# Attention with top-32 masking and two expert stages on one core: the first routed expert's slots in two passes, the first pass from the tokens of the first eight blocks

## The chip, the cores and the metric

The kernel runs on one core of a Trainium2 chip. The metric is the device time of one execution in microseconds (us). The engines are TensorE (PE in the rows, its weight loads PEld), VectorE (DVE), ScalarE (ACT), GpSimd (POOL) and SyncE (SP), which here only issues transfers.

## The reference, cut to what matters

Three stages follow one another on 2304 tokens of width 512. The change touches the third, and the end of the second.

```python
def _moe_ref(x, w_in, w_out):            # second stage, 2048 wide
    h = x @ w_in
    return (h * np.clip(h + 3, 0, 6) / 6) @ w_out

def _moe2_ref(x, w_gate, w1, w2):        # third stage: E = 8 experts, F = 1024
    logits = x @ w_gate
    expert_idx = np.argmax(logits, axis=1)
    gate_w = softmax(logits)[np.arange(N), expert_idx]
    for e in range(E):
        mask = expert_idx == e
        h = np.maximum(x[mask] @ w1[e], 0.0)
        out[mask] = gate_w[mask, None] * (h @ w2[e])
```

Each token goes to one expert alone. Which one is known only when the token's row of the second stage is complete.

## The kernel before, in words

**Tiling.** Tokens are worked in nine blocks of 256 (TB); each block has two tiles of 128. The main loop (lines 1075 to 1131) runs over attention tiles, and takes one step of the second stage in each turn. The second loop (lines 1143 to 1156) takes the steps that are left, without attention. A step (`moe_step`, line 1017) works on one of 16 slices of the hidden width of a block: `l1` (line 842) is 12 matmuls of 256 columns, `l2` (line 874), three steps behind, is 6 matmuls of 512 columns into the two banks `yps`. Every product is made of three matmuls, high by high, high by low, low by high. Between the two, ScalarE, VectorE and GpSimd make the activation and split it in two parts (`epi_a`, `epi_b`, `epi_c`); the parts gh and gl have two buffers each.

**Gates.** When a block's 16 steps are done, `yevac` (line 884) copies `yps` to two tiles `ysb` (three buffers), and a generator `gate` (line 893) per tile follows: four transposes and their copies, four small matmuls for the logits, the largest, its index, the one-hot row, a prefix count in its expert (lines 934 and 935), the token's row to DRAM (`yd`), and its number to a place in a table in DRAM (`td`, an indirect write of GpSimd, line 960). `gate_step` moves each generator one yield on; the loops call it once a turn. For the last block the table's entries are also made on chip (`place`, `in128`), and its indirect writes wait in a list, `tables`.

**Table and gather.** `load_table` reads the DRAM table back (`trow`) when the gates of the first 16 tiles are done. Behind the second loop, the counts give the experts' ranks (lines 1169 to 1175), and matmuls with `trow` and the last block's entries give `tab` and `tabg`: for each expert three slots of 128 token numbers (lines 1176 to 1185). Expert 0 always has the first rank; the others follow by count, and SP reads their numbers into registers (line 1189) for the addresses of their weights. `xgather` (line 1193) fetches the token rows of an expert by indirect reads of GpSimd, `xprep` (line 1204) transposes a slot's rows and splits them.

**Experts.** ROOM (line 98) says how many slots a rank has: 384, 384, 352, 320 three times, 256 twice. A step of an expert takes one of 8 slices (F = 1024): `m2l1` (line 1218) is 12 matmuls with as many columns as the rank has slots, `m2l2` (line 1239), two steps behind, 3 matmuls of 512 columns for each slot group. `m2out` scales, and writes the rows out by indirect writes. An expert's weights come as 8 pieces of 512 KB: `wload_` (line 985) loads one into one of three `raw` buffers, `wpiece` (line 998) splits it into a high part (ScalarE) and a low part (VectorE). Expert 0's first six pieces are loaded and split during the last 13 steps of the second stage; expert e + 1's piece f is asked for at step f of expert e.

**What sets the order.** The code doesn't write the order of each engine's queue out. Each instruction gets a priority number (`pr`, line 146: the turn's base and an offset by kind, gates 525, `l1` 310, `l2` 260, a turn is 400), and a planner builds every queue ahead of time: of the instructions whose inputs and buffers are there by the planner's own estimates, the one with the lowest number is next. On the chip a queue is worked in that order, and an instruction whose input is late holds up those behind it.

Of the kernel before, what the change touches and what calls it, by code (L numbers as in the profile page):

```python
# [57 lines left out]
def attention_two_moe_kernel(  # L58
# [38 lines left out]
    NSL = NE * SLOTS  # L97
    ROOM = [CAP, CAP, CAP - 32] + [CAP - 64] * 3 + [CAP - P] * 2

    def slots(r):  # L100
        return -(-ROOM[r] // P)

    def slot(r, j):
        return min(P, ROOM[r] - j * P)
    NCK = 8
# [114 lines left out]
    def body(cs, exact):  # L220
# [9 lines left out]
        m1p = m1.enter_context(tc.tile_pool(name="m1p" + X, bufs=1))  # L230
        ps1 = m1.enter_context(tc.tile_pool(name="ps1" + X, bufs=1, space=PSUM))
        at = ExitStack()
# [28 lines left out]

        wih = m1p.tile([P, NCC, F1], F32R, name="wih")
        wil = m1p.tile([P, NCC, F1], F32R, name="wil")

# [628 lines left out]
        def gate(bk, tt, y):  # L893
# [52 lines left out]
            if last:  # L946

                ad2 = m1p.tile([P, 1], I32, tag="ad2", bufs=2, name=f"ad2{i}")
                place, in128 = [wp[0].tile([P, n], F32, tag=f"oh{n}", bufs=2, name=f"oh{n}_{i}") for n in (P, NSL)]
# [26 lines left out]


        NPC = 4
        FW = F2 // NPC
# [18 lines left out]
        def wpiece(e, i):  # L998
            kind, pc = i % 2, i // 2
            if (e, i) not in wraw:  # L1000
                wload_(e, i)
            raw = wraw.pop((e, i))
            late = kind and pc >= NPC // 2
            nb = 3 if kind else 5
            pool = tabp[0] if late else wp[0]
            h = pool.tile([P, 4 * FW], F32R, tag=f"wh{kind}", bufs=nb, name=f"wh{e}_{i}")
            l = pool.tile([P, 4 * FW], F32R, tag=f"wl{kind}", bufs=nb, name=f"wl{e}_{i}")
# [135 lines left out]
        while gpos[0] < NG + 3 or pend:  # L1143
            pr0[0] += STEP
            run(moe_step())
            gate_step()
            tc.cur_priority = pr0[0] + STEP
            if gdone[0] == NTT - TB // P and not trows:
                load_table()
            if gpos[0] > NG - 13 and len(pre) < NPC + NPC // 2:  # L1150

                if len(wraw) == 3 or len(pre) + len(wraw) == NPC + NPC // 2:
                    pre.append(order[len(pre)])
                    wpiece(0, pre[-1])
                if len(pre) + len(wraw) < NPC + NPC // 2:
                    wload_(0, order[len(pre) + len(wraw)])
        m1.close()
# [4 lines left out]
        ps2 = m2.enter_context(tc.tile_pool(name="ps2" + X, bufs=1, space=PSUM))  # L1162
# [4 lines left out]
        rk = ps2.tile([P, 256], F32, name="rk")  # L1167
        cnt = rk[0:NSL, 0:NE]
        PE.matmul(cnt, ones[:, 0:NSL], ohsum, start=True, stop=True)
# [5 lines left out]
        V.tensor_scalar(place_, cs["row"][0:NSL, 0:NSL], rank[:, 2:3], None, op0=ALU.is_equal)  # L1175
        tq = ps2.tile([NSL, P], F32, tag="tp", bufs=2, name="tq")
        for i, a_ in enumerate(trows):
# [3 lines left out]
        V.scalar_tensor_tensor(trows[0], tq, part[:, 3:4], cs["row"][0:NSL, :], op0=ALU.subtract, op1=ALU.subtract)  # L1181
        tps = ps2.tile([P, NSL], F32, tag="tp", bufs=2, name="tps")
# [3 lines left out]
        PE.matmul(rk[0:1, 16:16 + NE], part[:, 1:2], place_.rearrange("p (e s) -> p e s", s=SLOTS)[:, :, 0], start=True, stop=True)  # L1186
        V.tensor_copy(cs["list"], rk[0:1, 16:16 + NE])
        for r in range(1, NE):
# [4 lines left out]
        def xgather(e):  # L1193
# [4 lines left out]
            for j in range(slots(e)):  # L1198
                x = tabp[0].tile([P, YW], F32, tag="xg", bufs=4, name=f"xg{e}_{j}")[0:slot(e, j)]
                G.indirect_dma_start(x, None, yd, bass.IndirectOffsetOnAxis(tabg[0:slot(e, j), e * SLOTS + j:e * SLOTS + j + 1], 0))  # L1200
                xg.append(x)
            xst[e] = (xh, xl, gw, xg)

        def xprep(e, j):
            xh, xl, gw, xg = xst[e]
            x = xg[j]
            m = slot(e, j)
            tp = ps2.tile([P, NCC, P], F32, tag="tp", bufs=2, name=f"tp{e}_{j}")[:, :, 0:m]
            for c in range(NCC):
# [8 lines left out]
        def m2l1(e, f):  # L1218
# [4 lines left out]
            fs = slice((f % FPP) * P, (f % FPP + 1) * P)  # L1223
            w = ROOM[e]
            lp = ps2.tile([P, CAP], F32, tag="lp", bufs=2, name=f"lp{e}_{f}")[:, 0:w]
# [10 lines left out]

        ops_ = [ps2.tile([P, DM], F32, name=f"ops{j}") for j in range(SLOTS)]

# [9 lines left out]
        def m2out(e):  # L1248
            gw = xst[e][2]
            for j in range(slots(e)):  # L1250
                m = slot(e, j)
                o = tabp[0].tile([P, DM], F32, tag="osb", bufs=3, name=f"osb{e}_{j}")[0:m]
                A.activation(o, ops_[j][0:m], AF.Copy, scale=gw[0:m, j:j + 1])
                si = G.indirect_dma_start(out, bass.IndirectOffsetOnAxis(tab[0:m, e * SLOTS + j:e * SLOTS + j + 1], 0), o, None,
                                          bounds_check=NT - 1, oob_is_err=False)
                tc.declare_no_dep(si.ins, group="out" + X, reason="no token is in two slots")
                tc.add_to_no_dep_group("out" + X, si.ins)

# [3 lines left out]
        for i in range(2 * NPC):  # L1262
            if i not in pre and (0, i) not in wraw:
                wload_(0, i, xst[0][3][0])
        for i in range(2 * NPC):
            if i not in pre:
                wpiece(0, i)
        for j in range(SLOTS):
            xprep(0, j)
        seq = [(e, f) for e in range(NE) for f in range(NF2)]  # L1270
        for s in range(len(seq) + 2):
            if s < len(seq):
                e, f = seq[s]
                if e + 1 < NE:
                    if f == (e == 0):
                        xgather(e + 1)
# [10 lines left out]
        m2.close()  # L1287


# [115 lines left out]
```

## Time and profile before

| | us |
|---|---|
| median of 3 runs (1209.82 to 1213.93) | 1211.6 |
| the profiled execution | 1211.3 |
| its span, first to last instruction | 1209.4 |
| TensorE busy | 1118.6 (92%) |
| VectorE busy | 934.9 (77%) |
| ScalarE busy | 809.0 (67%) |
| GpSimd busy | 459.0 (38%) |

All times in the rows count from the first instruction of the span. The span and the 1.9 us around it make the execution's time. A busy time says that an engine had something in hand, not that it set the end. Matmuls overlap each other, so a matmul's own duration is longer than the distance to the next; distances are read from starts, or from the pieces of the chain of waits.

### The profile page before, as it was taken

How to read it: one execution, taken by the hardware profiler on the slowest of the kernel's cores; microseconds unless marked ns; L12 is line 12 of the kernel's file. 1: busy time of each engine (PE TensorE's matmuls, PEld its weight loads, DVE VectorE, ACT ScalarE, POOL GpSimd, SP SyncE). 2: the span in 40 equal slices, each digit the busy share in tenths (PEclk: the TensorE clock that was granted, in tenths of full speed). 3: DMA queues.
4: the chain of work that ended last, by engine and by line, in shares of the span. 5: the costliest groups of instructions: out<-in, count | busy, mean ns of one | idle time of the engine just before them, and what ended most of it. 6: DMA issues, size and time to landing. Idle time of an engine off the chain costs nothing.

```text
span 1209.4 us, 24024 instructions
## 1 busy us (share of the span) xinstructions
PE 1118.6 (92%) x7410; PEld 999.2 (83%) x7410; DVE 934.9 (77%) x3821; ACT 809.0 (67%) x2085; POOL 459.0 (38%) x667
## 2 busy tenths in 40 slices
PE   5677688999999999999999999999998799999995
PEld 4566577788899899999988899999887699888894
DVE  4999999999999999998998899998442544444441
ACT  4787878788778788787777788777442444444441
POOL 5886655743322444422343332322353312112110
PEclk9678899999999999999999999999999799999998
DMA  3664566554544555743444554543583755555430
GB/s 77 198 182 135 171 200 209 143 157 135 152 127 127 134 145 154 169 140 114 124 127 139 117 151 134 129 144 103 172 258 109 217 173 175 155 180 185 145 104 17
DMA packets 184122, 179.23 MB, mean 148 GB/s; under 512 B 123629, under 2 KB 148509, under 8 KB 183984
## 3 DMA queue, kind: packets, MB, share of 16 engines
q1 hardware_dynamic: 178960, 167.24, 48.0%
q0 software_dynamic: 3872, 10.08, 2.5%
q8 instruction: 61, 1.00, 0.4%
q14 instruction: 77, 0.63, 0.2%
q10 hardware_dynamic: 1152, 0.28, 0.1%
HBM read 159.53 MB, written 18.61 MB: 147 GB/s over the span
## 4 chain that ended last, share of the span: by engine, by line
PE 74%; DVE 16%; ACT 5%; issue 2%; DMA 1%; POOL 1%; SPq 0%; ACTq 0%; POOLq 0%; DVEq 0%
PE l1ps L851 14%; PE yps L882 14%; PE ops L1246 10%; PE lp L1229 10%; PE ptps L777 9%; PE sps L618 5%; PE ptps L743 4%; DVE cd L648 2%; DVE pbuf L727 2%; DVE z L684 2%; DVE z L719 2%; PE ptps L910 1%; DVE cw L659 1%; DVE m L654 1%; PE misc L462 1%
## 5 line engine op out<-in xcount | busy, mean ns | idle before, releaser
L882 PE MATMUL yps<-wo,gh 128*128 128x512 f32 x576 | 216.5, 417 | 0.5 <-POOL qh L474 0.4
L286 POOL TENSOR_SCALAR gh<-gf 128x256 fp32r<-128x256 f32 x144 | 73.6, 511 | 343.6 <-PE yps L882 215.3
L648 DVE MAX8 cd<-sbuf 128x8 f32<-128x72 f32 x1152 | 187.9, 218 | 3.0 <-ACT sbuf L288 2.7
L851 PE MATMUL l1ps<-xh,wih 128*128 128x256 f32 x576 | 167.4, 291 | 4.5 <-DVE gf L863 2.4
L851 PE MATMUL l1ps<-xh,wil 128*128 128x256 f32 x576 | 163.8, 284 | 0.0
L851 PE MATMUL l1ps<-xl,wih 128*128 128x256 f32 x576 | 163.6, 284 | 0.0
L777 PE MATMUL ptps<-vn,pt 128*128 128x65 f32 (+1 forms) x1152 | 143.6, 278 | 0.0
L777 PEld LDWEIGHTS ptps<-vn,pt 128*128 128x128 f32 x1152 | 140.9, 198 | 0.0
L1009 DVE TENSOR_TENSOR wl<-raw,wh 128x1024 fp32r<-128x1024 f32 x64 | 78.3, 1231 | 79.6 <-ACT wh L1008 71.1
L727 DVE SCALAR_TENSOR_TENSOR pbuf<-sbuf,tall,pbuf 128x576 f32<-128x576 f32 x144 | 138.8, 964 | 0.1
L871 POOL TENSOR_TENSOR gl<-gf,gh 128x256 fp32r<-128x256 f32 x144 | 125.4, 871 | 11.4
L851 PEld LDWEIGHTS l1ps<-xh,wih 128*128 128x128 f32 x576 | 110.0, 191 | 15.2 <-DVE gf L863 7.2
L882 PEld LDWEIGHTS yps<-wo,gh 128*128 128x128 f32 x576 | 107.2, 189 | 16.7 <-POOL qh L474 0.9
L882 PE MATMUL yps<-wo,gl 128*128 128x512 f32 x288 | 116.8, 406 | 0.6 <-POOL gl L871 0.6
L709 ACT ACTIVATE jk<-sbuf,uall 128x576 bf16<-128x576 f32 x144 | 111.7, 775 | 4.2 <-DVE j L723 0.9
L700 ACT ACTIVATE pbuf<-sbuf,nb 128x576 f32<-128x576 f32 x144 | 111.1, 775 | 4.1 <-PE ptps L745 0.9
L851 PEld LDWEIGHTS l1ps<-xl,wih 128*128 128x128 f32 x576 | 110.1, 191 | 4.1
L288 ACT ACTIVATE sbuf<-sps 128x576 f32<-128x576 f32 x144 | 93.0, 646 | 28.8 <-PE sps L618 18.2
L1008 ACT ACTIVATE wh<-raw 128x1024 fp32r<-128x1024 f32 x64 | 67.3, 1059 | 66.1 <-PE lp L1229 31.7
L743 PE MATMUL ptps<-ident,pbuf 128*128 128x128 f32 x576 | 94.9, 288 | 17.6 <-DVE j L723 12.1
L857 ACT ACTIVATE gf<-l1ps,three 128x256 f32<-128x256 f32 x144 | 67.9, 472 | 64.1 <-PE l1ps L851 51.2
L851 PEld LDWEIGHTS l1ps<-xh,wil 128*128 128x128 f32 x576 | 110.4, 192 | 0.1
(237 smaller groups left out, 3006.1 us busy)
## 6 DMA issues: line engine op xcount, KB each, us to landing
wo<-wod SPq DMA_DIRECT2D x144, 512.0 KB, 3.8
raw<-in_moe_w_dram SPq DMA_DIRECT2D x64, 512.0 KB, 3.7
vn<-in_v_dram SPq DMA_DIRECT2D x96, 128.0 KB, 2.7
rawi<-in_moe_w_in_dram SPq DMA_DIRECT2D x16, 512.0 KB, 4.2
rawo<-in_moe_w_out_dram SPq DMA_DIRECT2D x16, 512.0 KB, 4.2
wod<-wc SPq DMA_DIRECT2D x16, 512.0 KB, 5.7
qn<-in_q_dram SPq DMA_DIRECT2D x126, 64.0 KB, 2.9
yd<-y SPq DMA_DIRECT2D x18, 258.0 KB, 5.0
```

The lines of the kernel that those rows point to most:

```text
L288: A.activation(dst, src, AF.Copy)
L648: V.max(cd[:, c, :], s[:, c * CK:(c + 1) * CK])
L700: A.activation(d["p"], d["s"], AF.Exp, bias=d["nb"], scale=SCALE)
L709: A.activation(jk, d["s"][:, 0:S], AF.Sign, bias=ts[t]["u"], scale=-1.0, accum_out=d["sg"])
L727: V.scalar_tensor_tensor(d["p"], d["s"], tall[:, t:t + 1], d["p"], op0=ALU.is_ge, op1=ALU.mult)
L743: PE.transpose(ptps[:, c * P:(c + 1) * P], pb[:, c0 + c * P:c0 + (c + 1) * P], ident)
L777: PE.matmul(d_, a_, b_, start=(i == 0), stop=(i == len(mm) - 1))
L851: PE.matmul(dst, a[:, c, fs], b_[:, c, :], start=(n == 0), stop=(n == 3 * NCC - 1))
L871: G.tensor_tensor(gl, gf, r_(gh), op=ALU.subtract)
L882: PE.matmul(yps[tt], a[:, tsl], b_, start=(f == 0 and m == 0), stop=(f == NF1 - 1 and m == 2))
L1229: PE.matmul(lp, a[:, c, fs], b_[:, c, 0:w], start=(n == 0), stop=(n == 3 * NCC - 1))
L1246: PE.matmul(ops_[j][0:slot(e, j)], a[:, js], b_[:, ns], start=(f == 0 and m == 0), stop=(f == NF2 - 1 and m == 2))
```

## The change

The first slots of expert 0 become a pass of their own. Its slots 0 to 255 (AHEAD = 2 groups) are filled only from the tokens of blocks 0 to 7. If expert 0 has fewer than 256 of those, its count is raised to 256 (`few`), so that the last block's tokens go to the third group in any case.

- `early_gather`, right after `load_table` in the second loop, makes the two groups' token numbers from `trow`, and fetches 2 x 128 rows into `ysb` buffers.
- `early_prep`, when all but one step of the second stage are issued, transposes and splits them in `sps` and the x buffers that block 8 doesn't use, and asks for expert 0's last two weight pieces.
- `early_l1` and `early_l2`, behind the table's instructions, are 8 steps of 12 matmuls of 256 columns and 6 of 512, in the banks `l1ps` and `yps` of the second stage.
- Expert 0's old pass stays for the third group alone: 128 columns in `m2l1`, one group in `m2l2`.
- In the second loop `gate_step` runs twice a turn while steps are left.
- Weight pieces have 4 buffers of each kind (before 5 and 6), and expert 1's piece i is split at step i + 4 of expert 0's third-group pass; so for all that follow, four steps later than before.
- The pool of the second stage's PSUM banks (`ps1`) is closed behind the first pass; `ps2`, the experts' banks, is opened there. The table's matmuls use `ptps`. `wih` and `wil` lie in a pool of their own, closed where `m1` was.

```diff
+    AHEAD = SLOTS - 1
+    def room(r):
+        return ROOM[r] - (r == 0) * AHEAD * P
+    def column(r, j):
+        return r * SLOTS + j + (r == 0) * AHEAD
...
+        def early_gather():
+            cps = misc([P, 1])
+            PE.matmul(cps, ones, ohsum[:, 0:1], start=True, stop=True)
...
+            ops0 = misc([P, AHEAD])
+            for i, a_ in enumerate(trows):
+                PE.matmul(ops0, a_, ident[0:NSL, 0:AHEAD], start=(i == 0), stop=(i == 1))
...
+            V.tensor_scalar(fg, ft, float(NT - TB - 1), None, op0=ALU.min)
...
+            for j in range(AHEAD):
+                x = m1p.tile([P, YW], F32, tag="ysb", bufs=NRAW, name=f"xa{j}")
+                G.indirect_dma_start(x, None, yd[0:NT - TB, :], bass.IndirectOffsetOnAxis(fg[:, j:j + 1], 0))
...
+        def early_prep():
+            xh, xl = xbuf[NBLK % 2]
...
+                tp = sps[:, j, :].rearrange("p (c q) -> p c q", c=NCC)
+                for c in range(NCC):
+                    PE.transpose(tp[:, c, :], x[:, c * P:(c + 1) * P], ident)
...
+                A.activation(xh[:, :, sl], tp, AF.Copy)
+                V.tensor_tensor(xl[:, :, sl], tp, r_(xh[:, :, sl]), op=ALU.subtract)
...
+        def early_l1(f):
...
+            lp = l1ps[:, f % 2, :]
+            n = 0
+            for c in range(NCC):
+                for a, b_ in ((h, xh), (h, xl), (l, xh)):
+                    PE.matmul(lp, a[:, c, fs], b_[:, c, :], start=(n == 0), stop=(n == 3 * NCC - 1))
+                    n += 1
+            hh = m1p.tile([P, TB], F32R, tag="gh", bufs=2, name=f"ha{f}")
+            hl = m1p.tile([P, TB], F32R, tag="gl", bufs=2, name=f"la{f}")
+            A.activation(hh, lp, AF.Relu)
+            V.scalar_tensor_tensor(hl, lp, 0.0, r_(hh), op0=ALU.max, op1=ALU.subtract)
...
+        def early_l2(f):
...
+            for j in range(AHEAD):
+                js = slice(j * P, (j + 1) * P)
+                for m, (a, b_) in enumerate(((hh, h), (hl, h), (hh, l))):
+                    PE.matmul(yps[j], a[:, js], b_[:, ns], start=(f == 0 and m == 0), stop=(f == NF2 - 1 and m == 2))
...
             gate_step()
+            if gpos[0] < NG:
+                gate_step()
...
                 load_table()
+                early_gather()
+            if gpos[0] >= NG - 1 and trows and "gw" not in ex_:
+                early_prep()
+                for i in order[len(pre) + len(wraw):]:
+                    wload_(0, i, ex_["x"][0])
...
         xgather(0)
         for f_ in tables:
             f_()
         for i in range(2 * NPC):
-            if i not in pre and (0, i) not in wraw:
-                wload_(0, i, xst[0][3][0])
-        for i in range(2 * NPC):
             if i not in pre:
                 wpiece(0, i)
-        for j in range(SLOTS):
-            xprep(0, j)
+        pieces = [(e, i) for e in range(1, NE) for i in range(2 * NPC)]
+        for i in range(2):
+            wload_(*pieces[i])
+        xgather(1)
+        for f in range(NF2 + 1):
+            if f < NF2:
+                early_l1(f)
+            if f:
+                early_l2(f - 1)
+            if f == NF2 - 1:
+                xprep(0, 0)
+        for j in range(AHEAD):
+            send(tabp[0].tile([P, DM], F32, tag="osb", bufs=3, name=f"osa{j}"), yps[j], ex_["gw"][:, j:j + 1], ex_["to"][:, j:j + 1])
+        m1s.close()
+        ps2 = m2.enter_context(tc.tile_pool(name="ps2" + X, bufs=1, space=PSUM))
...
-            if s < len(seq) and e + 1 < NE:
-                wpiece(e + 1, f)
+            if 4 <= s < len(pieces) + 4:
+                wpiece(*pieces[s - 4])
+            if 2 <= s < len(pieces):
+                wload_(*pieces[s])
```

`send` is `m2out`'s copy and indirect write, made a function of its own.

## Rows read from the trace of the kernel before

**Rows 1.** The page, 40 slices: TensorE busy in tenths, and its granted clock in tenths.

```profile
PE   5677688999999999999999999999998799999995
...
PEclk9678899999999999999999999999999799999998
```

**Rows 2.** Chain that ended last, 880 to 1010 us: start us, us, what.

```profile
922.79 4.20 PE yps L882 x18
...
944.77 1.10 PE tp L1210 x4
...
949.64 5.58 PE lp L1229 x24
...
980.94 2.08 PE lp L1229 x12
```

**Rows 3.** Busy time of the engines by stretch: PE, PEld, DVE, ACT, POOL, then PEclk.

```profile
930.00:940.00 10.00, 5.72 (x31) 3.93 (x31) 5.17 (x46) 2.09 (x10) 2.81 (x5) 0.59 0.16 54
940.00:950.00 10.00, 4.42 (x18) 3.51 (x18) 1.84 (x3) 2.11 (x4) 6.80 (x13) 0.50 0.81 219
950.00:960.00 10.00, 10.00 (x51) 9.37 (x50) 7.33 (x9) 6.81 (x9) 2.66 (x4) 0.89 0.92 305
```

**Rows 4.** TensorE weight loads in order of time, 896 to 897 us.

```profile
896.04 0.86 PEld L910 LDWEIGHTS ptps<-wg,yt 128*128 128x128 f32 x7
896.82 0.19 PEld L882 LDWEIGHTS yps<-wo,gh 128*128 128x128 f32 x1
896.93 0.19 PEld L882 LDWEIGHTS yps<-wo,gl 128*128 128x128 f32 x1
```

**Rows 5.** The same chain in block 8: a step with gate work, a step without.

```profile
889.65 0.57 PE ptps L910 x6
890.22 1.49 PE yps L882 x6
...
912.90 1.43 PE l1ps L851 x12
914.33 1.39 PE yps L882 x6
```

**Rows 6.** TensorE in order of time, 905 to 990 us, with idle time before.

```profile
934.92 0.18 PE L1169 MATMUL rk<-ohsum,ones 128*24 128x8 bf16 x1 [0.36 <-DVE lex L942]
935.03 1.04 PE L1178 MATMUL tq<-trow,ident 24*24 24x128 f32 x4
936.26 1.05 PE L1180 MATMUL tq<-oh,oh 128*24 128x128 f32 x4 [0.19 <-DVE oh L955]
```

**Rows 7.** ScalarE in order of time, 915 to 975 us.

```profile
927.01 1.08 ACT L889 ACTIVATE y<-yps 128x512 f32<-128x512 f32 x2 [3.66 <-PE yps L882]
```

**Rows 8.** TensorE in order of time at a tail tile, 211 us.

```profile
211.31 0.43 PE L618 MATMUL sps<-kx,qh 128*128 128x288 f32 x3
211.58 0.53 PE L618 MATMUL sps<-kx,ql 128*128 128x288 f32 x3
211.94 0.33 PE L813 MATMUL misc<-ident,xp 128*128 128x128 f32 x1
```

**Rows 9.** GpSimd in order of time, 885 to 950 us.

```profile
921.45 0.41 POOL L286 TENSOR_SCALAR gh<-gf 128x256 fp32r<-128x256 f32 x1 [1.60 <-PE yps L882]
921.94 0.74 POOL L871 TENSOR_TENSOR gl<-gf,gh 128x256 fp32r<-128x256 f32 x1
...
939.63 0.99 POOL L1200 DMA_INDIRECT xg<-yd,tabg  x1 [1.74 <-DVE list L1187]
```

**Rows 10.** Waits of the SP queue, 885 to 1010 us: us, times, longest.

```profile
SPq L975 <- DMA td<-tok,ad: 6.3, 2, 3.2
```

**Rows 11.** The page: DMA issues, median us to landing.

```profile
raw<-in_moe_w_dram SPq DMA_DIRECT2D x64, 512.0 KB, 3.7
...
yd<-y SPq DMA_DIRECT2D x18, 258.0 KB, 5.0
```

**Rows 12.** The page: conversion of expert weights on VectorE, busy us and mean ns.

```profile
L1009 DVE TENSOR_TENSOR wl<-raw,wh 128x1024 fp32r<-128x1024 f32 x64 | 78.3, 1231 | 79.6 <-ACT wh L1008 71.1
```

More of the change, by code (lines that the diff above doesn't have):

```diff
@@ L948, in gate @@
                 ad2 = m1p.tile([P, 1], I32, tag="ad2", bufs=2, name=f"ad2{i}")
-                place, in128 = [wp[0].tile([P, n], F32, tag=f"oh{n}", bufs=2, name=f"oh{n}_{i}") for n in (P, NSL)]
+                place = m1p.tile([P, TB], F32, tag="gf", bufs=2, name=f"place{i}")[:, 0:P]
+                in128 = wp[0].tile([P, NSL], F32, tag="in128", bufs=2, name=f"in128_{i}")
                 V.tensor_scalar(ad2, ad, P - 1, None, op0=ALU.bitwise_and)
@@ new lines, in early_prep @@
+        def early_prep():
+            xh, xl = xbuf[NBLK % 2]
+            gw = m1p.tile([P, AHEAD], F32, name="gwa")
+            ex_["gw"] = gw
+            for j, x in enumerate(ex_["x"]):
+                tp = sps[:, j, :].rearrange("p (c q) -> p c q", c=NCC)
+                for c in range(NCC):
+                    PE.transpose(tp[:, c, :], x[:, c * P:(c + 1) * P], ident)
+                sl = slice(j * P, (j + 1) * P)
+                A.activation(xh[:, :, sl], tp, AF.Copy)
+                V.tensor_tensor(xl[:, :, sl], tp, r_(xh[:, :, sl]), op=ALU.subtract)
+                G.tensor_copy(gw[:, j:j + 1], x[:, DM:DM + 1])
@@ new lines, in early_l1 @@
+        def early_l1(f):
+            xh, xl = xbuf[NBLK % 2]
+            h, l = [i.rearrange("p (c f) -> p c f", c=NCC) for i in wst[0, 0, f // FPP]]
+            fs = slice((f % FPP) * P, (f % FPP + 1) * P)
+            lp = l1ps[:, f % 2, :]
[8 more added lines that the diff above has]
+            V.scalar_tensor_tensor(hl, lp, 0.0, r_(hh), op0=ALU.max, op1=ALU.subtract)
+            ex_[f] = (hh, hl)
@@ L1002, in wpiece @@
             raw = wraw.pop((e, i))
[L1003 to L1007, printed above, removed]
+            h = wp[0].tile([P, 4 * FW], F32R, tag=f"wh{kind}", bufs=NPC, name=f"wh{e}_{i}")
+            l = wp[0].tile([P, 4 * FW], F32R, tag=f"wl{kind}", bufs=NPC, name=f"wl{e}_{i}")
             A.activation(h, raw, AF.Copy)
@@ L1166, in body @@
         rank = part[:, 4:8]
-        rk = ps2.tile([P, 256], F32, name="rk")
-        cnt = rk[0:NSL, 0:NE]
+        cnt = ptps[0:NSL, 0:NE]
         PE.matmul(cnt, ones[:, 0:NSL], ohsum, start=True, stop=True)
@@ L1175, in body @@
         V.tensor_scalar(place_, cs["row"][0:NSL, 0:NSL], rank[:, 2:3], None, op0=ALU.is_equal)
-        tq = ps2.tile([NSL, P], F32, tag="tp", bufs=2, name="tq")
+        tq = ptps[0:NSL, P:2 * P]
         for i, a_ in enumerate(trows):
@@ L1181, in body @@
         V.scalar_tensor_tensor(trows[0], tq, part[:, 3:4], cs["row"][0:NSL, :], op0=ALU.subtract, op1=ALU.subtract)
-        tps = ps2.tile([P, NSL], F32, tag="tp", bufs=2, name="tps")
+        tps = ptps[:, 2 * P:2 * P + NSL]
         PE.matmul(tps, trows[0], place_, start=True, stop=True)
@@ L1185, in body @@
         V.tensor_copy(tab, tps)
-        PE.matmul(rk[0:1, 16:16 + NE], part[:, 1:2], place_.rearrange("p (e s) -> p e s", s=SLOTS)[:, :, 0], start=True, stop=True)
-        V.tensor_copy(cs["list"], rk[0:1, 16:16 + NE])
+        by_rank = ptps[0:1, 3 * P:3 * P + NE]
+        PE.matmul(by_rank, part[:, 1:2], place_.rearrange("p (e s) -> p e s", s=SLOTS)[:, :, 0], start=True, stop=True)
+        V.tensor_copy(cs["list"], by_rank)
         for r in range(1, NE):
@@ L1207, in xprep @@
             m = slot(e, j)
-            tp = ps2.tile([P, NCC, P], F32, tag="tp", bufs=2, name=f"tp{e}_{j}")[:, :, 0:m]
+            tp = sps[:, 0, :].rearrange("p (c q) -> p c q", c=NCC) if e == 0 else \
+                ps2.tile([P, NCC, P], F32, tag="tp", bufs=2, name=f"tp{e}_{j}")[:, :, 0:m]
             for c in range(NCC):
@@ L1235, in m2l1 @@
             hst[e, f] = (hh, hl)
-        ops_ = [ps2.tile([P, DM], F32, name=f"ops{j}") for j in range(SLOTS)]
+        ops_ = []
         def m2l2(e, f):
@@ L1252, in m2out, with send @@
                 o = tabp[0].tile([P, DM], F32, tag="osb", bufs=3, name=f"osb{e}_{j}")[0:m]
[L1253 to L1257, printed above, removed]
+                send(o, ops_[j][0:m], gw[0:m, j:j + 1], tab[0:m, column(e, j):column(e, j) + 1])
+        def send(o, ps, gw, to):
+            A.activation(o, ps, AF.Copy, scale=gw)
+            si = G.indirect_dma_start(out, bass.IndirectOffsetOnAxis(to, 0), o, None, bounds_check=NT - 1, oob_is_err=False)
+            tc.declare_no_dep(si.ins, group="out" + X, reason="no token is in two slots")
+            tc.add_to_no_dep_group("out" + X, si.ins)
         xgather(0)
@@ L1262, in body @@
         for i in range(2 * NPC):
-            if i not in pre and (0, i) not in wraw:
-                wload_(0, i, xst[0][3][0])
-        for i in range(2 * NPC):
             if i not in pre:
                 wpiece(0, i)
-        for j in range(SLOTS):
-            xprep(0, j)
+        pieces = [(e, i) for e in range(1, NE) for i in range(2 * NPC)]
[13 more added lines that the diff above has]
+        ps2 = m2.enter_context(tc.tile_pool(name="ps2" + X, bufs=1, space=PSUM))
+        ops_.extend(ps2.tile([P, DM], F32, name=f"ops{j}") for j in range(SLOTS))
         seq = [(e, f) for e in range(NE) for f in range(NF2)]
@@ L1274, in body @@
                 if e + 1 < NE:
[L1275 removed]
+                    if f == 1 and e:
                         xgather(e + 1)
```

36 lines of the change are left out of this document (27 added, 9 removed).

## The prediction, made before the changed kernel ran

> **What bounds the kernel now.** I read the page's slices first, then the chain of waits across the end of the second stage, then the stretches around it. TensorE runs at its upper level, 2.4 GHz, nearly everywhere; the one dip behind the start lies in the 32nd slice, 937 to 968 us [rows 1]. The chain shows what happens there. The last matmuls of the second stage end at 922.79 + 4.20 = 926.99 us. Then the last block's gates, the table, the indirect writes and the gather of expert 0's rows follow one another, TensorE mostly waiting: its first transpose of gathered rows comes at 944.77, the first matmul of expert 0 at 949.64, and expert 1 begins at 980.94 [rows 2]. From there TensorE is full to the last slice [rows 1], and the other engines have room [rows 3], so what moves the start of expert 1 moves the end. Between 930 and 950 TensorE is busy 10.14 of 20 us, with a granted clock of 0.59 and 0.50, so at or near 1.2 GHz, and 0.89 in the ten us after that [rows 3].
>
> So the stretch to beat is 980.94 - 926.99 = 53.95 us. It holds expert 0's eight steps and some 20 us in which TensorE does little.
>
> **The change, priced.** I lay TensorE's work after the change end to end from 926.99 to the start of expert 1.
>
> *Put ahead of 926.99.* `early_prep` adds 8 transposes. A 128-column weight load follows the one before by 0.111 us (896.82 to 896.93, and seven loads in 0.78) [rows 4], and transposes and gate matmuls are no denser than their loads: 8 x 0.111 = 0.9. The count and the token numbers are five short passes, 0.4 at the same distance. TensorE has no gap in block 8, so these push all behind them: **1.3**. The second `gate_step` a turn adds no instruction; a tile's gate has nine parts and the second tile begins three turns behind, so block 7's gates need six turns of 2.82 us (1.43 + 1.39 [rows 5]) instead of twelve.
>
> *Gates and table, now between matmuls of the first pass.* 8 transposes and 16 logit matmuls at 0.111 are 2.7. The two groups of four table matmuls took 1.04 and 1.05 at the lower clock [rows 6]; at the upper one about half, 1.0. The handful of small ones 0.3. Sum **4.0**; at the lower clock it would be up to 8.
>
> *First pass.* Eight steps, each of 12 matmuls of 256 columns and 6 of 512, the same shapes as a step of block 8: 1.43 + 1.39 = 2.82 [rows 5], times 8 is **22.6**. In block 8 the six matmuls that follow gate work take 1.49 instead of 1.39 [rows 5]; for eight mixed steps I add **0.8**. The third group's four transposes add **0.4**.
>
> *Change of banks.* `ps2` opens where `ps1` closes. In the trace of before the first matmul into `ps2` (L1169) came when the last reader of `ptps` in `ps1` was done [rows 6], though it needs only counts; so the third group's first matmul may wait for both copies of `yps`. Two such copies took 1.08 [rows 7]; with the tail of the last matmul and the signals I take **1.4** (between nothing, if banks are waited for one by one, and 2.5).
>
> *Third group.* Eight steps of 12 matmuls of 128 columns: no such shape runs now. From below: at the column rate of the 512-column ones, 1.39 / 6 / 512 x 128 = 0.058. From above: 0.119, a 256-column one (1.43 / 12). That a short matmul of these operands costs more per column is excluded by a tail tile: 288, 224 and 64 columns follow one another in 211.31 to 211.58, so 0.27 for 576 columns, 0.47 ns each, as at 512. But in the second such group, 211.58 to 211.94, they take 0.36, about three times a weight load's distance [rows 8]. Each of the new matmuls has its own 128-column load, so I take 0.111 [rows 4]: 96 x 0.111 = 10.7. Six steps of one group's `m2l2` fall before expert 1 (3 x 0.231 each): 4.2. Expert 1's 12 transposes: 1.3. Together **16.2**.
>
> The Trainium skill (TensorE: Matmul & The Clock Gate, Back-to-back issue gap) gives about 81 ns a matmul for a stream of load and matmul pairs at 128 columns; by that the 96 would take 7.8 us, and the sum would come out 2.9 us shorter. The weight loads of this trace stand 111 ns apart, so I don't use it.
>
> Sum: 1.3 + 4.0 + 22.6 + 0.8 + 0.4 + 1.4 + 16.2 = 46.7, against 53.95. **Expert 1 starts 7.2 us earlier**, and so does the end. Against the profiled execution, 1211.3, that is 1204.1; the median of before is 0.3 above the profiled one: **1204.4**.
>
> **What I price at nothing, and its cover.** *GpSimd* gets the two early gathers in block 8, about 1 us each as a queue entry (as the one at 939.63), beside 0.41 and 0.74 of splitting in a step of 2.82 [rows 9]; the parts are made a step ahead of their `l2`, so an entry or two is absorbed. Without that cover each costs 1 us. *SP* waits at the table's read for the indirect writes, 3.2 us at the longest [rows 10], already now with loads of `wo` behind it that are asked for steps ahead; the same two waits come earlier. *The last y tile* needs the `ysb` buffer of the first early tile, which `early_prep` and a one-column copy for each late weight load have read by then. *Weights of expert 1:* SP can issue them only when the ranks are read, as now, around 940 to 945; three raw buffers take three pieces (3.7 us to landing each [rows 11]). The others wait for buffers that the third group's steps free one after another. Splitting costs VectorE 1.23 a piece [rows 12], with 1.33 to 2.5 us in a step. Piece 3 should be split by about 970 and is needed near 990, so 20 us of cover; the lead of later experts shrinks from eight steps to four, 11 us at the shortest steps (256 columns and two groups, as in block 8), against a landing of 3.7. *The third group's gather* now ends some 20 us behind the last matmul of block 8; its rows are needed at the first pass's last step, 25 us behind. If the table slips by 5 us that cover is gone, and TensorE waits.
>
> **Where a stall goes.** The 12 us or so of waits in gates, table, writes and gather stay in place, but with TensorE at work beside them; late next is the third group's gather, then expert 1's rows.
>
> **Rivals.**
>
> *A. Weight loads pass one another.* If a load begins well before the matmul ahead of it, the third group runs at its columns' rate: 96 x (0.111 - 0.058) = 5.1 less, **1199.3**. For it: the first group of the tail tile has three loads in 0.27, 0.09 each [rows 8]. Against: seven loads in 0.78 [rows 4]. The Trainium skill's 81 ns (same page and section) lies halfway.
>
> *B. The planner leaves the first pass behind the gates.* Then TensorE waits as now until the last block's entries are in, 936.26 + 1.05 = 937.31 [rows 6] or 10.3 us, the pass starts at the lower clock as expert 0 does now (10 us at 0.89, 1.1 lost [rows 3]), and the sum is 1.3 + 10.3 + 22.6 + 1.1 + 0.4 + 1.4 + 16.2 = 53.3, 0.65 earlier: **1211.0**, no difference. It decides if less than about half of the pass's first four steps lies ahead of the table. For it: all gate instructions have lower numbers, and only two l1 slices can go before `yps` is copied. Against: block 8's chain shows gate and stage matmuls merged with no gap [rows 5].
>
> *C. TensorE stands at an early read.* The token numbers need the table from DRAM, a few matmuls whose place in TensorE's queue the planner fixed by its own estimate of an indirect write, a read and a gather. If it thinks these fast, everything behind waits in block 8. Price, all of it: 3.2 for the write [rows 10], 5.0 for a landing on SP [rows 11] and 5.1 for gathered rows (from 939.63 [rows 9] to 944.77 [rows 2]), 13.3; less the gain of 7.2 it is 6.1 slower, **1217.7**. It decides from a stand of 10.8 us. For it: SP did stand 3.2 us behind these same writes. Against: block 7's gates end some five turns earlier, so by the same prices some 7 us lie between the gather's landing and `early_prep`; only the first matmuls on `trow` are without cover, 3 us or so. A stand of 3.5 to 10.8 us gives no measurable difference.
>
> *D. It doesn't keep to its slots.* If the last block had over 128 tokens for expert 0, the repair pass would run behind everything: eight weight pieces of 3.7 one behind another alone are 30 us, so 1230 or more. 32 are to be expected; chance 0.02.
>
> **How the numbers follow.** A measurement of this kernel tells about 0.3%, 3.6 us, from no change. The forecast itself 0.60, A 0.06: faster 0.66. B 0.13, and C's middle 0.09: within, 0.22. C in full 0.08, D 0.02, B with a late gather behind it 0.02: slower 0.12. The range takes in A (with a little idle left) and B: 1198.5 to 1213.5. The forecast's own range is 1199.3 to 1207.5.
>
> **What the profile after would show.** If right: TensorE at or near full between 927 and 957 with a clock of 1.0 and no dip in the 32nd slice; the first pass's `l1ps` matmuls 0.119 apart between gate matmuls; 128-column `lp` matmuls 0.111 apart; expert 1's first `lp` matmul near 973.7. Wrong by A: these stand 0.06 to 0.08 apart. By B: the dip is still there, and the first pass starts behind the table. By C: a gap of TensorE between 895 and 920, ended by `trow` or an early gathered row. A gap between the first pass and the third group of more than 2.5 us would show the banks or the third gather underpriced; gaps in expert 1, the weights.

## The result, and the profile after

The changed kernel takes **1222.66 us** (median of six, 1221.29 to 1225.58); the kernel before took 1213.83 in six runs (1209.82 to 1216.67). The ratio is **1.0082 [1.0059, 1.0105]**: slower, where 1204.4 and so a faster kernel was forecast, and above rival C in full (1217.7). The profiled execution took 1225.46, its span 1223.6.

The page after, TensorE busy and granted clock in 40 slices:

```profile
PE   5677788999999999999999999999988999999995
...
PEclk9688779999999999999999999999989999999998
```

The weak slices of [rows 1], the 31st and 32nd, are now the 30th and 31st, and the clock's dip is in the 30th, 887 to 918 us, where block 8 is worked. The table below takes marks from TensorE's instructions in order of time. All but the first column count from the start of block 8's first `l1`, except where said. "Third group" is the first `lp` matmul (in before: expert 0's first), "expert 1" is expert 1's first.

| us | block 8 starts at | last `yps` matmul | third group | expert 1 | from there to the last expert's last step | rest |
|---|---|---|---|---|---|---|
| before | 875.8 | 50.8 | 73.7 | 105.0 | 208.2 | 20.4 |
| after | 878.5 | 66.8 | 98.2 | 115.7 | 208.2 | 21.2 |

The spans differ by 14.2. Block 8 starts 2.7 later; across all the kernels profiled here it starts between 873.7 and 879.2 in no order that I can tie to the edits, so I leave that out. Of the rest, **block 8 lost 16.0** (forecast 1.3), the stretch from its last matmul to expert 1 gained 5.3 (54.2 to 48.9; forecast 8.5), and behind expert 1's start 0.8 was lost. So the place where the gain was sought did gain, and three times as much was lost just ahead of it. Four views show how. First TensorE after, in order of time (in brackets: idle before, and who ended it):

```profile
903.12 0.40 PE L892 MATMUL yps<-wo,gl 128*128 128x512 f32 x1
908.66 0.55 PE L1000 MATMUL misc<-ident,trow 24*128 24x2 f32 x2 [5.14 <-DMA trow<-td]
...
926.77 0.39 PE L861 MATMUL l1ps<-xh,wih 128*128 128x256 f32 x1 [2.29 <-DVE gf L873]
...
931.68 0.48 PE L861 MATMUL l1ps<-xh,wih 128*128 128x256 f32 x1 [1.83 <-DVE gf L873]
...
976.74 0.33 PE L1306 MATMUL lp<-xeh,wh 128*128 128x128 f32 x1 [1.36 <-ACT osa L1333]
976.90 0.27 PE L1306 MATMUL lp<-xel,wh 128*128 128x128 f32 x1
977.01 0.28 PE L1306 MATMUL lp<-xeh,wl 128*128 128x128 f32 x1
977.13 0.27 PE L1306 MATMUL lp<-xeh,wh 128*128 128x128 f32 x1
```

TensorE had no idle time in block 8 of before. Now it stands (idle, with the instruction at the head of its queue waiting for an input) 5.14 us at the first matmul that reads the table, and 2.29 and 1.83 us at two ordinary `l1` slices: 9.26 in all. What it waits for at the table, by the queues of GpSimd and then SP:

```profile
898.40 1.02 POOL L971 DMA_INDIRECT td<-tok,ad  x1 [0.62 <-DVE y L948]
901.00 1.01 POOL L971 DMA_INDIRECT td<-tok,ad  x1
```

```profile
906.32 0.83 SPq L986 DMA_DIRECT2D trow<-td  x1
...
907.70 0.72 SPq L986 DMA_DIRECT2D trow<-td  x1
```

```profile
SPq L986 <- DMA td<-tok,ad: 6.9, 1, 6.9
```

The same two queues in the kernel before:

```profile
903.58 1.02 POOL L960 DMA_INDIRECT td<-tok,ad  x1 [0.51 <-DVE ad L945]
```

```profile
907.84 0.84 SPq L975 DMA_DIRECT2D trow<-td  x1
```

There are two tables, one for each tile of a block, and a read waits for the writes of its own. The first read needs the write of 898.40, and SP could issue it only at 906.32: it waited 6.9, where its longest wait in [rows 10] was 3.2. From the write's issue to its read are 7.9 us; in the kernel before they were 4.3 (903.58 to 907.84). The second read, behind the write of 901.00, goes out at 907.70 without a further wait, and TensorE goes on at 908.66, 7.66 us behind that write. But in TensorE's queue the matmul stands right behind work that began at 903.12.

The two later gaps come from ScalarE's queue:

```profile
924.07 1.06 ACT L1078 ACTIVATE wh<-raw 128x1024 fp32r<-128x1024 f32 x1 [3.19 <-DMA raw<-in_moe_w_dram]
925.03 0.46 ACT L867 ACTIVATE gf<-l1ps,three 128x256 f32<-128x256 f32 x1
928.98 1.06 ACT L1078 ACTIVATE wh<-raw 128x1024 fp32r<-128x1024 f32 x1 [3.49 <-DMA raw<-in_moe_w_dram]
```

L1078 splits expert 0's last two weight pieces. Each split stands over 3 us for its load, and behind it stands L867, the activation that the next `l2` and, through the `l1ps` bank, the next `l1` need.

Last, the clock (columns as in [rows 3], the first being the stretch and its length; the granted clock comes behind the five engines):

```profile
903.00:907.90 4.90, 0.52 (x2) 0.08 (x1) 0.81 (x4) 0.47 (x1) 0.28 (x1) 1.00 0.00 0
907.90:914.80 6.90, 6.14 (x22) 5.46 (x23) 0.40 (x3) 0.13 (x1) 1.13 (x2) 0.51 0.48 158
914.80:931.80 17.00, 12.89 (x79) 10.90 (x78) 4.38 (x7) 4.14 (x7) 7.23 (x16) 1.00 0.67 229
931.80:935.20 3.40, 3.40 (x15) 3.21 (x16) 0.10 (x1) 0.47 (x1) 1.12 (x2) 0.50 0.24 92
935.20:975.00 39.80, 39.50 (x250) 33.41 (x248) 11.28 (x60) 9.58 (x27) 10.73 (x20) 1.00 0.33 94
```

Behind the stand TensorE works 6.14 us at 0.51, the level of 1.2 GHz, and behind the last gap 3.40 at 0.50: half of both, 4.8, is lost. Together 9.26 + 4.8 + the 1.3 that was forecast = 15.4 of the 16.0. From 935.20 on the first pass runs as forecast, 39.5 of 39.8 us busy at a clock of 1.00.

### The profile page after: what moved, and what is told of

Same layout as the page of the kernel before. It is cut to its first block, busy times and chain, and to the rows that moved or that the text cites. A ratio compares the mean times of both kernels' runs of the same rounds, so it can differ in the third digit from the quotient of the medians.

```text
span 1223.6 us, 24240 instructions
## 1 busy us (share of the span) xinstructions
PE 1129.4 (92%) x7511; PEld 1008.7 (82%) x7511; DVE 934.7 (76%) x3835; ACT 806.6 (66%) x2093; POOL 463.9 (38%) x667
## 5 line engine op out<-in xcount | busy, mean ns | idle before, releaser
L1079 DVE TENSOR_TENSOR wl<-raw,wh 128x1024 fp32r<-128x1024 f32 x64 | 78.5, 1226 | 105.3 <-ACT wh L1078 103.2
L1078 ACT ACTIVATE wh<-raw 128x1024 fp32r<-128x1024 f32 x64 | 67.7, 1058 | 88.9 <-PE lp L1306 58.7
L867 ACT ACTIVATE gf<-l1ps,three 128x256 f32<-128x256 f32 x144 | 67.8, 471 | 71.5 <-PE l1ps L861 55.9
```

## The experiments

In each table row below the columns are those of the first table. In the diffs a line of "..." leaves code out; e0 is a diff against the kernel before, the others against the changed kernel unless another is named.

**e0, a second gate step a turn in the kernel before.**

```diff
             gate_step()
+            if gpos[0] < NG:
+                gate_step()
```

> Kernel before with the second gate_step a turn alone. Theory (two in-order waits cost the time): no early read and no late weight piece here, so within 2 us of the kernel before, TensorE full through block 8. Rival (the doubled gate work or its earlier table read already slows block 8): 3 us or more slower, with gaps of TensorE between 880 and 927.

Measured: 1215.41 against 1215.07, 1.0007 [0.9988, 1.0027]. Block 8's last `yps` matmul came at 53.5, 2.7 later than in before; TensorE's two waits in it were for `wo`, one of them this:

```profile
912.35 0.47 PE L882 MATMUL yps<-wo,gh 128*128 128x512 f32 x1 [1.01 <-DMA wo<-wod]
```

So the crowded gates alone cost no time that a measurement can tell, though they are not quite free in this profile. They do delay the table. GpSimd's first write, then SP's first read:

```profile
898.32 1.02 POOL L960 DMA_INDIRECT td<-tok,ad  x1 [0.28 <-DVE y L938]
```

```profile
907.93 0.84 SPq L975 DMA_DIRECT2D trow<-td  x1
```

That is 9.6 us from write to read, against 4.3 in the kernel before. In the other kernels with the second gate step whose read is not tied to a later step (after, e1, e2, e3, e8) it is 7.5 to 8.1. So the second gate step brings the write forward and lengthens the time until the read can go; by what, is not shown.

**e1, the table's matmuls asked for two turns behind the table's read.**

```diff
                 load_table()
-                early_gather()
+                tread[0] = gpos[0]
+            if trows and not ex_ and gpos[0] >= tread[0] + 2:
+                early_gather()
```

> Changed kernel, the first use of the table on TensorE two turns (5.6 us) behind the read. Theory: the 5.1 us gap at L1000 goes, and the half clock behind it (908 to 915, some 3 us): 7 to 9 us faster than the changed kernel's 1222.7, so 1214 to 1216; the two gaps behind ScalarE (2.3 and 1.8) stay. Rival (the wait only moves: the gather lands late and early_prep's transposes wait instead): 1220 to 1223, a gap of some 5 us at the transposes of the early rows.

Measured: 1218.28, 1.0041 [1.0018, 1.0064]. The stand is smaller and not gone:

```profile
912.62 0.58 PE L1001 MATMUL misc<-ident,trow 24*128 24x2 f32 x2 [3.08 <-DMA trow<-td]
...
925.46 0.38 PE L861 MATMUL l1ps<-xh,wih 128*128 128x256 f32 x1 [0.18 <-DVE gf L873]
```

Block 8 took 58.8 instead of 66.8. The late weight pieces, which follow the gather, were shifted too, and the second kind of gap shrank with them, so this run alone doesn't separate the two. At 1218.28 it is above the 1214 to 1216 expected.

**e2, all eight pieces of expert 0 loaded and split ahead of the table, none behind it.**

```diff
                 early_prep()
-                for i in order[len(pre) + len(wraw):]:
-                    wload_(0, i, ex_["x"][0])
-            if gpos[0] > NG - 13 and len(pre) < NPC + NPC // 2:
+            if gpos[0] > NG - 13 and len(pre) < 2 * NPC:
...
```

> Changed kernel, expert 0's last two weight pieces loaded and split in the same run as the first six, not behind the early gather. Theory: the splits no longer stand on ScalarE (3.2 and 3.5 us) ahead of the second stage's activations, the gaps of 2.3 and 1.8 us at L861 and the half clock of 932 to 935 go: 5 to 6 us faster than the changed kernel, 1216.5 to 1218; the gap at the table read stays. Rival (the two gaps come from GpSimd or from the 1 MB more on the DMA engines): no faster than 1221.

Measured: 1218.19, 1.0042 [1.0018, 1.0066]; block 8 61.4. The gaps at `l1` are gone, the stand at the table is there in two parts:

```profile
904.82 0.58 PE L1000 MATMUL misc<-ident,trow 24*128 24x2 f32 x2 [3.29 <-DMA trow<-td]
...
907.92 0.58 PE L1000 MATMUL misc<-ident,trow 24*128 24x2 f32 x2 [1.16 <-DMA trow<-td]
```

So the pieces cause the gaps at `l1` and not the one at the table. New here: the third group's matmuls ran at half clock for 10.2 us, which they did not in the changed kernel:

```profile
969.00:979.20 10.20, 10.20 (x45) 9.51 (x44) 3.01 (x5) 3.65 (x7) 0.13 (x1) 0.50 0.22 79
```

**e3, the edits of e1 and e2 together.**

> Changed kernel with both edits. Theory: the gains add up, 12 to 15 us off 1222.7: 1208 to 1211, so below the kernel before by 3 to 6 us; block 8 as long as before plus 1.3 us; expert 1 starts 3 to 5 us earlier than before (the forecast's 7.2, less what the third group's own waits cost). Rival (the change cannot gain, since what is taken out of the stretch behind block 8 is given back in it): 1214 or more.

Measured: 1216.69, 1.0030 [1.0010, 1.0049]; block 8 60.6. The two gains did not add up. TensorE's gaps:

```profile
911.61 0.57 PE L1001 MATMUL misc<-ident,trow 24*128 24x2 f32 x4 [1.83 <-DMA trow<-td]
...
916.88 0.58 PE L861 MATMUL l1ps<-xh,wih 128*128 128x256 f32 x1 [1.89 <-DVE gf L873]
```

ScalarE, and SP's queue:

```profile
913.92 1.06 ACT L1079 ACTIVATE wh<-raw 128x1024 fp32r<-128x1024 f32 x1 [6.96 <-DMA raw<-in_moe_w_dram]
```

```profile
907.04 2.12 SPq L986 DMA_DIRECT2D trow<-td  x2
909.26 1.74 SPq L1069 DMA_DIRECT2D raw<-in_moe_w_dram  x1
```

A weight load stood on SP behind the table's read, the read behind the indirect write, the split on ScalarE behind the load, and the activations behind the split. The first wait moved from TensorE's queue to two others.

**e4, the table's read and its first matmul each tied to a later step.** The planner places an instruction where it thinks its inputs are there. So each gets an input that is late for certain: one column of `trow` is written by GpSimd from a tile of two steps ago, and the first matmul reads a copy of the identity slice, touched in the same way two turns later.

```diff
+            for a_ in trows:
+                G.tensor_copy(a_[:, 0:1], after[0:NSL, 0:1])
...
+            few2 = m1p.tile([NSL, AHEAD], F32, name="few2")
+            G.tensor_copy(few2[:, 0:1], after[0:NSL, 0:1])
+            G.tensor_copy(few2, ident[0:NSL, 0:AHEAD])
...
-                PE.matmul(ops0, a_, ident[0:NSL, 0:AHEAD], start=(i == 0), stop=(i == 1))
+                PE.matmul(ops0, a_, few2, start=(i == 0), stop=(i == 1))
...
+            if tdone[0] and not trows and gpos[0] >= tdone[0] + 2:
+                tread[0] = gpos[0]
+                load_table(gst[gpos[0] - 2])
```

> Changed kernel; the table's read is tied to a second-stage activation two turns later, and the first matmul on it to one two further turns on, so neither SP nor TensorE should reach them before the data is there. Theory (in-order waits on the DRAM table): SP waits under 1 us for the indirect writes (6.9 before), TensorE under 0.5 us at the table rows, no half clock around 910; the two late weight pieces still stand on ScalarE and cost up to 3 us; block 8 (from its first l1 to the last yps matmul) 54 to 58 us, where the changed kernel took 66.8 and the kernel before 50.8. Time 1214 to 1217. Rival (the rows land late whatever the order, since the small reads queue behind 512 KB loads): a wait of 2 us or more at the table rows stays.

Measured: 1213.64 against 1213.34, 1.0002 [0.9990, 1.0015]; block 8 56.9, so 9.9 of the 16.0 are back. TensorE no longer waits for `trow`, and its clock in block 8 stays up. SP still waits 1.9 for the writes, where under 1 was expected. Left is the second kind, and a wait for early transposes (TensorE, then ScalarE):

```profile
922.34 0.66 PE L1026 MATMUL sps<-ident,xa 128*128 128x128 f32 x4 [1.94 <-DVE xl L1029]
...
928.48 0.39 PE L1040 MATMUL l1ps<-xh,wh 128*128 128x256 f32 x1 [1.60 <-DVE gf L873]
```

```profile
919.37 1.06 ACT L1084 ACTIVATE wh<-raw 128x1024 fp32r<-128x1024 f32 x1 [3.20 <-DMA raw<-in_moe_w_dram]
...
925.78 1.06 ACT L1084 ACTIVATE wh<-raw 128x1024 fp32r<-128x1024 f32 x1 [2.15 <-DMA raw<-in_moe_w_dram]
```

**e5, e4 with the pieces of e2, and the early transposes two turns later.**

> As e4_touch, with all eight weight pieces of expert 0 in one run and the early rows transposed two turns later. Theory: no wait over 0.5 us of TensorE in block 8, which takes 52 to 53.5 us (before 50.8, plus 1.3 for the added matmuls, plus little); expert 1 starts 101 to 103 us behind block 8's first l1 (105.0 before, 115.7 in the changed kernel); 1.5 to 4 us below the kernel before, 1210 to 1213 where that shows 1214 to 1215. Rival (something else than the waits on the table and the pieces lengthens block 8, such as the doubled gate work or the DMA load): block 8 stays over 56 us, and the time at or above the kernel before.

Measured: 1218.28, 1.0030 [1.0014, 1.0046]; block 8 58.8, worse than e4. The pieces now collide ahead of the table instead of behind it (ScalarE, then TensorE):

```profile
906.41 1.06 ACT L1084 ACTIVATE wh<-raw 128x1024 fp32r<-128x1024 f32 x1 [5.24 <-DMA raw<-in_moe_w_dram]
```

```profile
909.11 0.58 PE L861 MATMUL l1ps<-xh,wih 128*128 128x256 f32 x1 [4.41 <-DVE gf L873]
```

And the third group ran at 1.2 GHz for 17.0 us: 24.4 to expert 1, where the changed kernel took 17.5. Loading earlier was no cure here. That the planner takes a load for shorter than it is, is argued from this; its estimates are not in the record.

**e8, the two late splits alone tied to the first pass's first activation, the table as in the changed kernel.**

```diff
+            if after is not None:
+                copy(True, h[:, 0:1], r_(after[:, 0:1]))
             A.activation(h, raw, AF.Copy)
...
+            if f == 0:
+                for i in range(2 * NPC):
+                    if i not in pre:
+                        wpiece(0, i, ex_[0][0])
```

> Changed kernel; only the splits of expert 0's last two weight pieces are tied to the first pass's first activation, so ScalarE cannot stand on their loads in block 8. Theory (ScalarE's two waits of 3.2 and 3.5 us hold up the second stage's activations): the gaps of 2.3 and 1.8 us at L861 and the half clock of 932 to 935 go, the one of 5.1 us at the table read stays; block 8 58 to 62 us instead of 66.8; 4 to 6 us faster than the changed kernel's 1222.7. Rival (the gaps come from the table's read being late, and go only with it): within 2 us of 1222.7.

Measured: 1219.18 against 1213.55, 1.0063 [1.0041, 1.0086]; block 8 59.8. The table's stand remains, alone:

```profile
908.64 0.55 PE L1000 MATMUL misc<-ident,trow 24*128 24x2 f32 x2 [5.30 <-DMA trow<-td]
```

Taken out of the changed kernel alone, the two late pieces are worth 66.8 - 59.8 = 7.0 of block 8, and the table's stand with its clock 66.8 - 56.9 = 9.9 (e4). That is 16.9, against 14.7 for both at once in the next run (e6, 52.1): the two losses overlap. Taken out second they are worth 4.8 (e4 to e6) and 7.7 (e8 to e6). By times e8 gained less than its profile: it is 5.6 above the kernel before, where the changed kernel was 8.8 above, so 3.2, under the 4 to 6 expected.

**e6, e4 and e8 together.**

> e4_touch with the same tie, so both waits gone. Theory: TensorE waits under 1 us in block 8, which takes 51.8 to 53.5 us; expert 1 starts 100.5 to 102.5 us behind block 8's first l1 (105.0 in the kernel before), if the clock stays up in the third group; 2.5 to 4.5 us below the kernel before. Rival (the late pieces only move the wait: early_l2 of step 4 then stands on them): a gap of 2 us or more in the first pass, and no gain on the kernel before.

Measured: 1211.46 against 1213.55, 0.9979 [0.9959, 1.0000]. Block 8 took 52.1: **50.8 of before, plus the 1.3 that the prediction put there.** But the third group lost its clock, 2.6 us after its start:

```profile
962.30:964.90 2.60, 2.56 (x23) 2.56 (x23) 0.29 (x1) 0.28 (x1) 1.73 (x2) 1.00 0.45 174
964.90:975.10 10.20, 10.20 (x45) 9.51 (x43) 4.08 (x6) 4.33 (x7) 0.24 (x1) 0.50 0.24 79
975.10:983.50 8.40, 8.40 (x63) 7.79 (x63) 5.14 (x9) 3.75 (x7) 3.14 (x3) 1.00 0.73 243
```

TensorE is busy without a gap when the clock falls, though 1.36 us of waiting stood just ahead of the group. The group took 21.2 instead of 17.5.

**e9, e6 with the second of the two `yps` copies on VectorE**, to shorten the wait of 1.36 for the banks that stands just ahead of that fall.

```diff
-            send(tabp[0].tile([P, DM], F32, tag="osb", bufs=3, name=f"osa{j}"), yps[j], ...
+            send((A, V)[j], tabp[0].tile([P, DM], F32, tag="osb", bufs=3, name=f"osa{j}"), yps[j], ...
```

> e6_tied with the second of the two yps copies on VectorE, beside ScalarE's. Theory (the third group's first matmul waits for both copies, since the experts' banks open only when the second stage's are all read): the gap ahead of the third group falls from 1.36 to 0.6 to 0.9 us; expert 1 starts 0.5 to 0.8 us earlier against the last yps matmul than in e6_tied at the same clock; 2 to 4 us below the kernel before. Rival (the gap is set by something else, the gathered rows or the transposes): it stays at 1.3 or more.

Measured: 1211.08 against 1211.78, 0.9977 [0.9958, 0.9996]. The wait did not shrink, it is 1.56 and now ends with VectorE's copy; the clock was down for 17.1 us, and matmuls of 128 columns stood 0.213 apart:

```profile
960.10 0.33 PE L1318 MATMUL lp<-xeh,wh 128*128 128x128 f32 x1 [1.56 <-DVE osa L1348]
...
972.96 0.41 PE L1318 MATMUL lp<-xel,wh 128*128 128x128 f32 x1
973.18 0.41 PE L1318 MATMUL lp<-xeh,wl 128*128 128x128 f32 x1
973.39 0.41 PE L1318 MATMUL lp<-xeh,wh 128*128 128x128 f32 x1
```

```profile
961.30:978.40 17.10, 17.10 (x74) 16.02 (x73) 5.46 (x9) 5.48 (x10) 1.88 (x2) 0.50 0.39 130
```

The edit did not set the copies beside each other. VectorE's waited for ScalarE's to end:

```profile
959.30 0.75 DVE L1348 TENSOR_SCALAR osa<-yps,gwa 128x512 f32<-128x512 f32 x1 [0.77 <-ACT osa L1346]
```

So whether copies side by side would shorten the wait was not tested. The gap alone does not decide the clock: in the changed kernel it was 1.36 as in e6, and the clock stayed up.

**e10, e9 with each of the third group's `l1` matmuls streaming its 128 columns twice.** Nobody reads the second half; it is extra work, and nothing of the computation is left out.

```diff
+            lpw = lpt[:, 0:2 * w].rearrange("p (a w) -> p a w", a=2) if e == 0 else None
...
+                    if e == 0:
+                        PE.matmul(lpw, a[:, c, fs], b_[:, c, 0:w].unsqueeze(1).to_broadcast([P, 2, w]), start=(n == 0), stop=(n == 3 * NCC - 1))
```

> As e9_split, but each of the third group's first-layer matmuls streams its 128 columns twice (256 columns, same weight loads; the second half is left unread). Theory (these matmuls are held by their weight loads): 0.117 to 0.12 us apart as with 128 columns, the third group no longer than in e9_split (17 to 17.5 us while the clock is up). Rival (columns set their pace, so the forecast's lower bound of 0.058 is what 128 columns could reach): 96 x 0.058 = 5.6 us longer.

Measured: **1206.37** (1205.21 to 1208.12) against 1211.78, **0.9940 [0.9917, 0.9962]**. It is faster than the kernel before, and than e9 in the same session (1211.08). The doubled matmuls stand 0.12 apart, where those of 128 columns stood 0.112, the gap ahead is the same 1.56, and the clock stays at 1.00:

```profile
961.74 0.39 PE L1321 MATMUL lp<-xeh,wh 128*128 128x256 f32 x1 [1.56 <-DVE osa L1353]
...
970.57 0.28 PE L1321 MATMUL lp<-xeh,wl 128*128 128x256 f32 x1
970.69 0.28 PE L1321 MATMUL lp<-xeh,wh 128*128 128x256 f32 x1
970.81 0.28 PE L1321 MATMUL lp<-xel,wh 128*128 128x256 f32 x1
```

```profile
900.00:961.70 61.70, 59.48 (x379) 50.88 (x377) 17.80 (x75) 15.36 (x37) 24.48 (x49) 1.00 0.56 157
961.70:979.00 17.30, 17.24 (x127) 16.07 (x128) 9.53 (x16) 8.48 (x17) 6.02 (x5) 1.00 0.52 186
```

All kernels by stretch, in the columns of the first table:

| us | block 8 starts at | last `yps` matmul | third group | expert 1 | to the last step | rest |
|---|---|---|---|---|---|---|
| e0 | 878.5 | 53.5 | 77.2 | 109.3 | 208.2 | 20.4 |
| e1 | 878.5 | 58.8 | 90.5 | 108.0 | 208.4 | 21.0 |
| e2 | 874.3 | 61.4 | 92.8 | 114.0 | 207.4 | 21.1 |
| e3 | 879.2 | 60.6 | 91.9 | 109.4 | 207.8 | 20.9 |
| e4 | 874.0 | 56.9 | 87.7 | 105.3 | 208.0 | 21.3 |
| e5 | 873.7 | 58.8 | 90.5 | 114.9 | 207.3 | 21.0 |
| e8 | 878.3 | 59.8 | 91.9 | 109.4 | 208.3 | 21.1 |
| e6 | 878.2 | 52.1 | 84.1 | 105.3 | 207.4 | 21.0 |
| e9 | 876.0 | 51.8 | 84.1 | 108.5 | 207.3 | 20.9 |
| e10 | 877.7 | 51.8 | 84.0 | 101.3 | 206.3 | 21.0 |

## Why the prediction was wrong

**The step that failed** is the paragraph "Against" of rival C: "some 7 us lie between the gather's landing and `early_prep`; only the first matmuls on `trow` are without cover, 3 us or so", with a chance of 0.17 for C in all. The mechanism was named with its place and its sign (a gap between 895 and 920, ended by `trow`) and dismissed by its price. There are two errors in the price. The stand is 5.14, not 3. I took the write at 3.2 from SP's longest wait in [rows 10], but SP came to that wait about 1 us behind the write's issue: from issue to read it was 4.3 in the kernel before already. In the changed kernel it is 7.9 (898.40 to 906.32), and the read added 2.3 more. Under "Put ahead" the second `gate_step` was said to add no instruction, and nothing was put down for it; yet counted from block 8's start it brings the write 7.9 us forward (27.8 to 19.9) and the read only 4.2 (32.0 to 27.8), and e0 shows the same with this edit alone. And I let TensorE resume at its upper level, although [rows 3] had shown 0.50 to 0.59 where TensorE stood again and again; that is another 3.1. In block 8 the stand with its clock is worth 7.7 (e8 to e6) to 9.9 (after to e4), most of the 10.8 from which C was to decide.

The Trainium skill (DMA: Bandwidth & Descriptors, Anatomy of one DMA — SWDGE (gpsimd) path) puts a fixed 2 us or so on a transfer that GpSimd issues. An estimate from it that gives SP's read as much, write and read one behind the other, is 4 us from 901.00, a stand of some 1.5; the trace has 7.66 from that write to the matmul, and the measurement decides.

**A term that was missing.** Under "What I price at nothing" stand expert 1's pieces and their landing, but not expert 0's two late ones: I looked at the load's buffer and not at the queue of the engine that splits it. ScalarE stood 3.19 + 3.49 in front of block 8's activations, TensorE 2.29 + 1.83, with 1.7 of clock behind it; e8 gives 7.0 of block 8 for all of it, e4 to e6 4.8. GpSimd and SP were examined for such stands; ScalarE, which the change also gives an early instruction with a late input, was not.

**Terms that were mis-sized.** From the last `yps` matmul to the third group the sum has 4.0 + 22.6 + 0.8 + 0.4 + 1.4 = 29.2; measured were 31.4 after and 32.2 in e10. Counted in after from each start to the next, the matmuls of gates and table took 4.7 (for 4.0), and the first pass's own 24.6 without the wait for the banks (for 22.6 + 0.8): 0.133 from a matmul of 256 columns to what comes next, instead of 0.119. The third group took 17.5 (e10 17.3) for 16.2.

**What was right.** Block 8's own added work: 52.1 in e6 against 50.8 is the 1.3 (e9 and e10: 51.8). Matmuls of 128 columns stand 0.112 apart (0.111 forecast), so rival A falls. The Trainium skill's 81 ns (TensorE: Matmul & The Clock Gate, Back-to-back issue gap) does not hold for these pairs of load and matmul; the measurement decides. The change of banks took 1.36 (1.4), and it ends with the second copy of `yps` as named, also in e9, where that copy is VectorE's. The first pass was placed among the gates, so rival B falls: 39.5 of 39.8 us busy. Nothing moved behind expert 1 (208.2 in both). And the gain sought is real once the waits are out of block 8: e10 starts expert 1 at 101.3, 3.7 earlier than before, which is the 7.2 less 3.0 up to the third group and 1.1 in it, but for 0.6. By the times e10 gains 0.6%, [0.4%, 0.8%]; another 1.9 comes behind expert 1's start, which I didn't follow further.

**What stays open.** Why the clock falls in the third group of e2, e5, e6 and e9, and not in after, e1, e3, e4 and e8, was not settled: the matmuls are the same, and each kernel has one profile. That twice the columns hold it up is supported, not shown: five of the nine profiles with 128 columns kept the clock too, and e10 has one profile and four times. These lie within 3 us (1205.21 to 1208.12), where e6 and e9 spread over 11.6 (1205.13 to 1216.73, 1205.24 to 1216.77); only two of e9's twelve runs are as fast as e10's slowest. The spread goes with the clock: e9's fastest run had a mean granted clock of 0.973, its slowest 0.958. But in what stage is not on record, and the kernel before, without this group, spread over 7.9 in the same session, 1209.79 at 0.963 to 1217.70 at 0.954. Whether e9's copy is needed in e10 wasn't tried.

## What to carry to other kernels

Where a planner builds each engine's queue ahead of time, work that is moved early takes its inputs' true delay with it: follow every input that comes from DRAM to the engine that consumes it, count from the issue of the first transfer to the landing of the last, and ask what stands behind the consumer in its queue, on every engine that gets one. Count in the order that the change makes, not in the old one: here a second gate step alone more than doubled the time from write to read (4.3 to 9.6, e0). Asking earlier or later by a fixed number of turns only made a wait smaller or moved it (e1, e2, e3, e5); tying the consumer to something that is late for certain took it out (e4, e8, e6). To a stand of TensorE add the slow stretch behind it that the profile shows.

## What the runs showed of the hardware that I had not expected

The granted clock fell from 1.00 to 0.50 while TensorE was busy without a gap (e6: 2.56 of 2.60 us busy before the fall, behind a gap of 1.36), in a stream of 128-column matmuls with a 128-column load each; it stayed there for 10.2 to 17.1 us, and the matmuls stood 0.213 apart instead of 0.112. In the one profile with 256 columns per load the same stream took 0.12 a matmul and kept its clock. By these distances the doubled columns cost about 0.8 us in 96 matmuls (an estimate, 96 x 0.008); the whole group took 17.3, against 17.5 in after and 24.4 in e9.

An indirect write of 128 numbers took 7.9 us from its issue until the read behind it could go, 9.6 in e0 and 4.3 in the kernel before; a 512 KB weight load took 3.7 in [rows 11]. In after the DMA engines moved nothing from 903.00 to 907.90 (share 0.00, 0 GB/s), so its last 3.3 us were not spent behind moving data.
